# A list-scheduled attention-plus-feed-forward kernel: later landings in the planner, one more weight pair prepared during attention

## The chip, the cores and the metric

The kernel runs on one core of a Trainium2 chip. The metric is the device time of one execution in microseconds. The kernel before takes 1083.32 us (median of three runs, 1082.94 to 1085.74).

The engines are named as the profile names them: PE is the matrix engine (PEld its weight loads), DVE the vector engine, ACT the scalar engine, POOL the GpSimd engine, SP the engine whose queue issues nearly all transfers. Each executes its own instructions strictly in the order in which they stand in the program and waits on semaphores for the others.

## The reference

```python
scores = scale * np.matmul(q, k.transpose(0, 1, 3, 2))     # 8 batches x 8 heads, 576 positions, 64 wide
mask = block_i >= block_j                                  # blocks of 64: block-causal
attn = softmax(np.where(mask, scores, -1e9))
x = np.matmul(attn, v)                                     # reshaped to 4608 tokens x 512
h = x @ w_in                                               # 512 -> 2048
g = np.maximum(h, 0.0) + alpha * np.minimum(h, 0.0)        # one alpha per column of w_in
out = g @ w_out                                            # 2048 -> 512
```

The inputs q, k and v are float32. The two weight matrices arrive as float64 bit patterns and are turned into float32 on the chip.

## The kernel before, in words

**Arithmetic.** Every float32 operand of a matrix product is split into a rounded high part and a low rest (`split`, and `QH`/`QL`, `KH`/`KL`, `gh`/`gl`, `xh`/`xl`), and a product is made of three passes on PE: high by high, high by low, low by high.

**Two stages.** The 2048 hidden columns are 16 slices of 128. In the first stage, up to about 560 us, the attention of 32 head pairs is done (`query_tile` for scores, softmax and transposes, `values` for the product with v), and beside it `chunk_a` takes the finished tokens through the first six slices (`FA = 6`; `ffn1` at L638, `activate` at L649 to L659, `ffn2` at L672) in chunks of 256 tokens. After the last attention tile some chunks of `chunk_a` remain; they fill PE until about 628 us. In the second stage the other ten slices are done as five pairs by a scheme of seven instead of eight block products (`pair1` at L736, `chunk2` at L794). It needs seven combinations ("factors") of the 256 by 256 blocks of each pair of weight slices, high and low parts of each. This is what "pair" means for weights below: (1, g) are the W2 factors of pair g, from w_out, and (0, g) the W1 factors, from w_in.

**Weights.** `to_f32` loads 512 KB of float64 bits into a buffer `raw` (two exist) and makes float32 of them in a buffer `m` (two exist beside the attention) with one operation on ACT (L495) and five on DVE (L492, L497, L501, L504, L507). For the first six slices the result is split into `wa` and stays on chip. For the five pairs, `weights_ahead(p)` does it beside the attention after head pair p: two conversions, four block sums on DVE (L530), four splits on ACT (L557) and POOL (L558), and eight transfers (L562) that write the factors to DRAM (`wd` for W2, `wd1` for W1). The buffers `m` and `raw` are free again only when these transfers have landed. The table `AHEAD` says at which head pair which factors are made; its priority is `5*p + WOFF`. Pair (0, 0) is not in the table: its W1 factors are made at the change of stages, on ACT and POOL, from buffers on chip (`later_weights`); for the other four a load of 896 KB per part (L594) brings them back from DRAM.

**Order.** No order is written by hand. `Plan.op` records each operation with an engine, a cost, its buffers and a priority (lower is sooner). `Plan.schedule` is a list scheduler: it plays the program through with these costs, gives each free engine the ready operation with the lowest priority, and the order in which it does so is the order of the instructions on each engine. For a transfer it assumes that issuing takes `ISSUE`, that data begin to move `BEGINS` later, one transfer after the other at `PER_KB`, and that it has landed `LANDS` after that. What is planned too early then waits in order at run time, and all that stands behind it on that engine waits too. `slack` adds time to one operation before the next may use its result, but for transfers it is overwritten. The planned times decide order alone; the chip does not see them.

**The start.** For the first four head pairs q and k of the first 256 positions are loaded into regions of `xT` (L931, L932), k is scaled on DVE (L917) or POOL (L919), and the scores come directly from them (L1002). Values `vraw` come by L938.

Of the kernel before, what the change touches and what calls it, by code (L numbers as in the profile page):

```python
# [9 lines left out]
F32 = mybir.dt.float32  # L10
# [18 lines left out]
NG = (NF - FA) // 2  # L29
# [8 lines left out]
HALVES = (((4, 3, 2), (2 * P, S, 1)), ((1, 0), (0, 2 * P, 0)))  # L38
BANKS, HB, AB, HT, AM, AT, WB = 7, 2, 2, 5, 2, 3, 4
SLACK = 0  # L40
# [3 lines left out]
STARTS1, STARTS2 = (5, 22, 34, 46, 58), (0, 12, 17, 29, 41, 53, 65)  # L44
C0, C1 = 3.0, 4.0
WARM, WARM_END = 10, 3400
TICK, FULL_COLUMNS = 3413.33, 3060
LAG = 7.25
NORM, GL, XLA, KON = ("POOL",) * 5, ("POOL",) * 4, ("POOL",) * 2, "POOL"
W1A, W1L, WAA, WAL = ("POOL",) * 4, ("POOL",) * 4, "DVE", "POOL"  # L50
Q2B = 1
VP, VL, VE = 2.0, 2.0, 0.0
E0, E1 = -4.0, 2.0
RAW0, FIXED = -9.4, 3
NEAR, LP = 4.0, 1.0
FP = -1
# [3 lines left out]
ON_DVE, D0 = (3,), 12  # L60
WOFF, COFF = 100, 60
AHEAD = {**{8 + 4 * k: (1, k) for k in range(NG)}, **{6 + 4 * k: (0, k) for k in range(1, NG)}}
CONV = {}
SHIFTS = {}
SOON, XB = 150, 1006.7
FEW = 12
# [9 lines left out]
       ("POOL", "SP"): 120}  # L76
HELD, PACE = {"DVE": 40, "POOL": 80}, 1.012
QUEUES = ("SP", "ACTQ", "POOLQ")
ISSUE, BEGINS, LANDS, PER_KB, LANES = 430, 1300, 1000, 4.1, 8

# [19 lines left out]
class Plan:  # L100
# [45 lines left out]
    def schedule(self):  # L146
# [44 lines left out]
        while events:  # L191
# [13 lines left out]
            for engine in sorted(ready, key=lambda e: (e in ("DVE", "POOL"), since.get(e, t), ready[e][0] if ready[e] else (0, 0))):  # L205
# [54 lines left out]
                if engine in QUEUES:  # L260
                    begin = max([t, *lands[-LANES:][:len(lands) >= LANES]])
                    end = begin + ISSUE
                    pipe = max(begin + BEGINS, pipe) + cost * PER_KB
                    lands.append(pipe + LANDS)
                    lat = lands[-1] - end
                busy[engine] = end
# [90 lines left out]
def attn_ffn(ctx, tc, qT, kT, vT, w_in, w_out, alpha, out):  # L357
# [120 lines left out]
    def to_f32(src, prio, after=(), use="att", early=None):  # L478
# [9 lines left out]
        def e():  # L488
            return eb().bitcast(I32)
        op("SP", 512, lambda: nc.sync.dma_start(out=raw(), in_=src), r=after, w=[raw], prio=prio if early is None else early)  # L490

# [43 lines left out]
    def weights_ahead(p):  # L535
# [18 lines left out]
        def parts(src, n, keys, at):  # L554

            n2 = 256 * n
            op("ACT", c_act(n2, True), lambda: nc.scalar.copy(out=word(2, n).bitcast(F32R), in_=src()), r=keys, w=[hk], prio=pr)  # L557
            op(WAL, c_pool(n2) if WAL == "POOL" else c_ss(n2), lambda: (nc.gpsimd if WAL == "POOL" else nc.vector).tensor_tensor(  # L558
                out=src().bitcast(F32R), in0=src(), in1=word(2, n), op=ALU.subtract), r=[hk], w=keys, prio=pr)
            for x, v, r in ((0, lambda: word(2, n), [hk]), (1, src, keys)):  # L560
                to = wd[at:at + n, :, g, x].rearrange("m p n -> p m n") if side else wd1[g, :, x, at:at + n]
                op("SP", 128 * n, lambda to=to, v=v: nc.sync.dma_start(out=to, in_=v().rearrange("p (m n) -> p m n", n=256)),  # L562
                   r=r, w=[("wd", side, at + i, g, x) for i in range(n)], prio=pr)
        if side:
# [308 lines left out]
    def store(acc, to, t, key):  # L873
        o = Buf("o")
        op("ACT", c_act(512), lambda: nc.scalar.copy(out=o(), in_=acc()), r=[acc], w=[o], prio=FP)
        op("SP", 256, lambda: nc.sync.dma_start(out=to[t:t + P, :], in_=o()), r=[o], w=[(key, t)], prio=FP)

# [5 lines left out]
    def prep(p, pr):  # L883
# [3 lines left out]
        QH, QL, KH, KL, Q, K = (Buf(k) for k in ("QH", "QL", "KH", "KL", "Q", "K"))  # L887
        op("SP", 320, lambda: nc.sync.dma_start(out=raw(), in_=qT[p]), w=[raw], prio=pr)
        op("SP", 288, lambda: nc.sync.dma_start(out=kraw(), in_=kT[p]), w=[kraw], prio=pr)
        op("SP", 320, lambda: nc.sync.dma_start(out=vraw(), in_=vT[p]), w=[(vraw, 0), (vraw, 1)], prio=pr + VL)  # L890
        v_parts = vraw, [(vraw, 0), (vraw, 1)]
# [10 lines left out]
        def move(to, of, key, src, kb=128):  # L902
            op("SP", kb, lambda: nc.sync.dma_start(out=to().bitcast(F32), in_=of().bitcast(F32)), r=[src], w=[key], prio=pr)
        for h in range(2):
# [239 lines left out]
    def spill(b, pr):  # L1144
        r0 = (b * S) % RING
        n = S
        op("SP", 2 * n, lambda: nc.sync.dma_start(out=xd[:, :, b * S:b * S + n], in_=xT[:, :, r0:r0 + n]),
           r=xs(b), w=[("xd", b)], prio=pr)

# [14 lines left out]
    for p in range(NPAIR):  # L1164
        pr = p * 5
        qk_parts, v_parts = prep(p, pr - 4.5) if p >= NP else rest(p, pr - 4.5)
        halves = HALVES[:1] if p < NP else HALVES
        js = [j for js, _ in halves for j in js]
        for k, j in enumerate(js):
            query_tile(p, qk_parts, j, pr + k)  # L1170
        values(p, v_parts, [span for _, span in halves], pr + len(js) + VAL)
        weights_ahead(p)
        if p % NP == NP - 1:
            b = p // NP
            spill(b, p * 5 + 20)
# [114 lines left out]
```

## Time and profile before

| | |
|---|---|
| median of three runs | 1083.32 us |
| profiled execution: own time / span in the trace | 1084.71 us / 1082.9 us |
| PE idle over the span | 18.9 us (1082.9 less 1064.0 busy) |
| first matmul of the scores | 5.93 us |
| last attention product, first matmul of the second stage | 563 us, 628.65 us |
| transfers | 248 MB, 229 GB/s on average |

A row of the view of windows gives, for a stretch, its length and then for each engine the busy time and the number of instructions, then the granted clock of PE, the busy share of the sixteen DMA engines and their rate. A row of the timeline gives start, duration, engine, line, operation, output and inputs, count, and in brackets how long the engine had been idle and what released it. A row of waits gives who waited for whom, microseconds in total, how often, and the longest.

### The profile page before, as it was taken

The numbers are of one execution on the slowest core, as the hardware profiler recorded it, in microseconds if no ns is written. First come the engines' busy times: TensorE is split into PE (matmuls) and PEld (weight loads), VectorE is DVE, ScalarE is ACT, GpSimd is POOL, SyncE is SP. The second block draws the span as 40 slices with busy tenths as digits, with TensorE's granted clock in tenths as the row PEclk, the third lists the DMA queues.
The fourth block names the chain that finished last, engine by engine and source line by source line (L and its number), as shares of the span: only waits on it lengthen the run. The fifth ranks groups of instructions, "written<-read, shape, count | busy, mean of one in ns | idle before, by whom it ended". The sixth has DMA issues, their size and how long they took to land.

```text
span 1082.9 us, 24707 instructions
## 1 busy us (share of the span) xinstructions
PE 1064.0 (98%) x8158; PEld 964.8 (89%) x8158; DVE 769.5 (71%) x1731; ACT 704.1 (65%) x1977; POOL 686.9 (63%) x877
## 2 busy tenths in 40 slices
PE   7999999999999999999999999999999999999998
PEld 4678887888888887888888999999999999999998
DVE  7887775857675757686767259687777869686865
ACT  6889987676767666676754446556565656565553
POOL 4767857566767556667556616675767666675741
PEclk9999999999999999999999999999999999999999
DMA  6598988768877769668547367787877879686974
GB/s 193 185 248 240 260 253 226 244 176 235 241 214 236 198 211 272 207 191 267 161 159 288 107 253 224 224 275 230 265 249 238 268 218 285 214 286 211 296 259 156
DMA packets 150224, 248.07 MB, mean 229 GB/s; under 512 B 15952, under 2 KB 62800, under 8 KB 150096
## 3 DMA queue, kind: packets, MB, share of 16 engines
q1 hardware_dynamic: 149520, 245.96, 73.9%
q8 instruction: 65, 1.06, 0.4%
q14 instruction: 63, 0.52, 0.2%
q10 hardware_dynamic: 576, 0.52, 0.1%
HBM read 157.56 MB, written 44.83 MB: 187 GB/s over the span
## 4 chain that ended last, share of the span: by engine, by line
PE 85%; DVE 6%; ACT 4%; DMA 3%; issue 1%; POOL 1%; SPq 0%; DVEq 0%; ACTq 0%; POOLq 0%
PE bank L794 20%; PE bank L736 20%; PE bank L638 12%; PE bank L672 12%; PE bank L1134 7%; PE bank L1035 5%; PE bank L997 5%; DMA raw<-in_w_in 2%; PE bank L1065 2%; PE bank L1090 1%; ACT p L1021 1%; DVE nm L1018 1%; DVE bank L497 1%; ACT PTF L1110 1%; DMA wd<-m 0%
## 5 line engine op out<-in xcount | busy, mean ns | idle before, releaser
L736 PE MATMUL bank<-X,w 128*128 128x256 f32 x1890 | 245.6, 282 | 0.7 <-ACT g L745 0.7
L736 PEld LDWEIGHTS bank<-X,w 128*128 128x128 f32 x1890 | 233.6, 189 | 1.3 <-ACT g L745 1.1
L794 PE MATMUL bank<-w,gh 128*128 128x256 f32 x1260 | 229.2, 280 | 0.8 <-ACT gh L513 0.8
L514 POOL TENSOR_TENSOR gl<-c,gh 128x256 fp32r<-128x256 f32 x175 | 150.6, 873 | 82.6 <-ACT gh L513 64.1
L968 POOL TENSOR_SCALAR p<-p,ri 128x256 f32<-128x256 f32 (+3 forms) x256 | 142.8, 571 | 94.7 <-DVE ri L1027 51.2
L794 PEld LDWEIGHTS bank<-w,gh 128*128 128x128 f32 x1260 | 193.9, 189 | 1.0 <-ACT gh L513 1.0
L794 PE MATMUL bank<-w,gl 128*128 128x256 f32 x630 | 177.2, 281 | 0.0
L1021 ACT ACTIVATE p<-bank,nm 128x256 f32<-128x256 f32 (+3 forms) x256 | 134.6, 535 | 47.5 <-DVE nm L1018 30.2
L672 PE MATMUL bank<-wa,gh 128*128 128x512 f32 x432 | 140.5, 406 | 0.5 <-POOL wa L514 0.5
L638 PE MATMUL bank<-xh,wa 128*128 128x256 f32 x864 | 129.1, 288 | 0.3 <-ACT PTF L1110 0.3
L794 PEld LDWEIGHTS bank<-w,gl 128*128 128x128 f32 x630 | 118.9, 189 | 0.0
L659 POOL TENSOR_TENSOR gl<-g,gh 128x256 fp32r<-128x256 f32 x108 | 83.0, 770 | 55.5 <-ACT gh L655 47.2
L638 PEld LDWEIGHTS bank<-xh,wa 128*128 128x128 f32 x864 | 113.5, 190 | 3.5 <-ACT PTF L1110 0.9
L1035 PE MATMUL bank<-ident,p 128*128 128x128 f32 x640 | 100.7, 278 | 7.5 <-POOL p L968 3.2
L753 ACT ACTIVATE g<-bank 128x256 f32<-128x256 f32 x135 | 51.6, 384 | 82.7 <-DVE bank L749 67.7
L513 ACT CAST gh<-c 128x256 fp32r<-128x256 f32 x192 | 76.4, 406 | 35.4 <-PE bank L794 31.5
L1134 PE MATMUL bank<-PTF,vraw 128*64 128x320 f32 (+3 forms) x768 | 94.8, 386 | 0.0
L1035 PEld LDWEIGHTS bank<-ident,p 128*128 128x128 f32 x640 | 74.6, 142 | 21.0 <-POOL p L968 9.4
L997 PE MATMUL bank<-K,Q 128*128 128x512 f32 (+1 forms) x448 | 92.4, 327 | 0.1
L1018 DVE TENSOR_REDUCE nm<-bank 128x1 f32<-128x384 f32 (+3 forms) x144 | 81.0, 587 | 15.2 <-PE bank L997 7.8
L672 PEld LDWEIGHTS bank<-wa,gh 128*128 128x128 f32 x432 | 75.0, 189 | 12.6 <-POOL wa L514 0.8
L672 PE MATMUL bank<-wa,gl 128*128 128x512 f32 x216 | 85.2, 394 | 0.0
(180 smaller groups left out, 2135.6 us busy)
## 6 DMA issues: line engine op xcount, KB each, us to landing
w<-wd SPq DMA_DIRECT2D x315, 256.0 KB, 4.0
Q<-QH SPq DMA_DIRECT2D x56, 256.0 KB, 3.8
K<-KH SPq DMA_DIRECT2D x112, 128.0 KB, 3.5
vraw<-in_v SPq DMA_DIRECT2D x32, 320.0 KB, 4.2
qraw<-in_q SPq DMA_DIRECT2D x30, 320.0 KB, 4.0
xd<-xT SPq DMA_DIRECT2D x8, 1152.0 KB, 6.8
part<-o SPq DMA_DIRECT2D x36, 256.0 KB, 3.6
wd<-raw SPq DMA_DIRECT2D x36, 256.0 KB, 3.5
```

The source lines that it names most:

```text
L514: op(on, c_pool(n) if on == "POOL" else c_ss(n), lambda: (nc.gpsimd if on == "POOL" else nc.vector).tensor_tensor(out=lo(), in0=src(), in1 ...
L638: nc.tensor.matmul(hp()[:, :n], ww()[:, 0, cc * P:(cc + 1) * P], x()[:, cc, :n], start=(i == 0 and cc == 0), stop=(i == 2 and cc == NCC - 1))
L659: op(on, c_pool(CHA) if on == "POOL" else c_ss(CHA), lambda: (nc.gpsimd if on == "POOL" else nc.vector).tensor_tensor(out=gl(), in0=g(), i ...
L672: nc.tensor.matmul(acc(), a()[:, ts], ww(), start=(first and i == 0), stop=(last and i == 2))
L736: nc.tensor.matmul(bank()[:, :CHA], W()[:, i, 256 * at + P * c:256 * at + P * c + P], B()[:, j, CHA * c:CHA * c + CHA], start=(first and n ...
L794: nc.tensor.matmul(bank()[:, CHA * i:CHA * i + CHA], a()[:, P * i:P * i + P], W()[:, x], start=(first and g + i + n == 0), stop=(g == NG - ...
L968: op(on, 244 + n / 1.2 if on == "POOL" else c_dve2(n), lambda: e.tensor_scalar(out=t()[:, cols], in0=t()[:, cols], scalar1=by(), scalar2=1 ...
L997: nc.tensor.matmul(o, Q()[:, i, qs], K()[:, 2 * h + i, :w], start=(i == 0), stop=(i == 1))
L1018: op("DVE", c_dve(w), lambda h=h: nc.vector.tensor_reduce(out=nm()[:, h:h + 1], in_=sb[h]()[:, off[h]:off[h] + w], axis=AX.X, op=ALU.max, ...
L1021: op("ACT", 238 + w / 1.2, lambda h=h, t=t: nc.scalar.activation(out=t()[:, :w], in_=sb[h]()[:, off[h]:off[h] + w], func=AF.Exp, bias=nm() ...
L1035: nc.tensor.transpose(out=tp()[:, base + c * P:base + (c + 1) * P], in_=pts[h]()[:, c * P:(c + 1) * P], identity=ident)
L1134: nc.tensor.matmul(ob()[rows[h], a - q0:q1 - q0], V()[:, c, h, :], moving, start=(c == 0), stop=(c == cs[-1][0]))
```

## The change

Constants of the planner and of the placement, and one term in the planner's treatment of transfers:

- A transfer now lands `LANDS = 2000` after its data instead of 1000, and a transfer's `slack` is added. `LATE[1] = 2000` is the slack of the factors that go out (L562), `LATE[4] = 3000` that of the stored partial sums (L876) and of the attention's spilled result (L1147); the other three entries are zero. For a factor block of 256 KB the planner thus counts 1300 + 256 x 4.1 + 1000 = 3350 ns from the start of the issue before, and 1300 + 1050 + 2000 + 2000 = 6350 ns now.
- `AHEAD` holds all ten factor sets. The first is made after head pair 6 instead of 8. `WOFF` goes from 100 to 0, so that a conversion has the priority of the attention tiles of its time instead of one that comes behind all of them.
- The fourth entry of `GL` is DVE: for slice 3 of the first six, the low part `gl` is made on DVE instead of POOL (18 of 108 such operations).
- Loads of a head pair have priority `5*p - 5.5` instead of `- 4.5`, values no longer two later. `E0`, `E1`, `C0`, `C1`, `XB`, `SOON` move the first tiles, the first six slices' weights and the first loads of the second stage. `HT` lets four instead of five hidden banks be in use once the attention ends.

```diff
-BANKS, HB, AB, HT, AM, AT, WB = 7, 2, 2, 5, 2, 3, 4
+BANKS, HB, AB, HT, AM, AT, WB = 7, 2, 2, 4, 2, 3, 4
-C0, C1 = 3.0, 4.0
+C0, C1 = 6.0, 3.0
-NORM, GL, XLA, KON = ("POOL",) * 5, ("POOL",) * 4, ("POOL",) * 2, "POOL"
+NORM, GL, XLA, KON = ("POOL", "POOL", "POOL", "POOL", "POOL"), ("POOL", "POOL", "POOL", "DVE"), ("POOL", "POOL"), "POOL"
-VP, VL, VE = 2.0, 2.0, 0.0
-E0, E1 = -4.0, 2.0
+VP, VL, VE, PP = 3.0, 0.0, 0.0, 5.5
+E0, E1 = -3.0, 0.6
-WOFF, COFF = 100, 60
-AHEAD = {**{8 + 4 * k: (1, k) for k in range(NG)}, **{6 + 4 * k: (0, k) for k in range(1, NG)}}
+WOFF, COFF = 0, 60
+AHEAD = {6: (1, 0), 8: (0, 0), 10: (1, 1), 12: (0, 1), 15: (1, 2), 17: (0, 2), 19: (1, 3), 22: (0, 3), 24: (1, 4), 26: (0, 4)}
-SOON, XB = 150, 1006.7
+SOON, XB = 140, 1004.7
+LATE = (0, 2000, 0, 0, 3000)
-ISSUE, BEGINS, LANDS, PER_KB, LANES = 430, 1300, 1000, 4.1, 8
+ISSUE, BEGINS, LANDS, PER_KB, LANES = 430, 1300, 2000, 4.1, 8
@@ schedule @@
-                    lat = lands[-1] - end
+                    lat = lands[-1] - end + lat
@@ weights_ahead, parts @@
-                   r=r, w=[("wd", side, at + i, g, x) for i in range(n)], prio=pr)
+                   r=r, w=[("wd", side, at + i, g, x) for i in range(n)], prio=pr, slack=LATE[1])
@@ store; spill likewise @@
-        op("SP", 256, lambda: nc.sync.dma_start(out=to[t:t + P, :], in_=o()), r=[o], w=[(key, t)], prio=FP)
+        op("SP", 256, lambda: nc.sync.dma_start(out=to[t:t + P, :], in_=o()), r=[o], w=[(key, t)], prio=FP, slack=LATE[4])
@@ attn_ffn @@
-        qk_parts, v_parts = prep(p, pr - 4.5) if p >= NP else rest(p, pr - 4.5)
+        qk_parts, v_parts = prep(p, pr - PP) if p >= NP else rest(p, pr - PP)
```

One line is added near the top, so that line numbers of the changed kernel are one higher below it. On PE the last 3541 matmuls, from about 658 us on, stand in the same order in both kernels.

**First place: the first transfers on SP.** Before:

```order
L938 DMA vraw_156<-in_v 128x256
L938 DMA vraw_159<-in_v 128x256
L932 DMA xT<-in_q 128x256 x3
L931 DMA xT<-in_k 128x256
L932 DMA xT<-in_q 128x256
L490 DMA raw_169<-in_w_in 128x1024
```

Now:

```order
L933 DMA xT<-in_q 128x256 x3
L932 DMA xT<-in_k 128x256
L933 DMA xT<-in_q 128x256
L491 DMA raw_164<-in_w_in 128x1024
L939 DMA vraw_166<-in_v 128x256
L939 DMA vraw_169<-in_v 128x256
```

The two loads of values have moved from the head of the queue to behind the first load of weights; the first q is now the first transfer.

**Second place: ACT around the second use of `m` by the first factor set (1, 0).** `m_242` is the first of the two buffers in both; `CAST raw<-m` splits a factor out of it, and the next `ACTIVATE bank<-m` works on the following conversion in the same buffer. Before:

```order
L898 CAST KH_716<-kraw_171 128x576
L1021 ACTIVATE p_201,s_133<-bank_194,nm_204 128x512
L1021 ACTIVATE p_207,s_133<-bank_176,nm_204 128x512
L557 CAST raw_169<-m_293 128x512
L495 ACTIVATE bank_231<-m_242,ebias 128x512
L1138 COPY xT<-bank_145 128x320
L1110 COPY PT_109<-bank_194 64x128
```

Now:

```order
L876 COPY o_1307<-bank_231 128x512
L558 CAST raw_164<-m_344 128x512
L1111 COPY PTF_108<-bank_190 128x4x128
L1111 COPY PTF_108<-bank_180 128x4x128
L1111 COPY PTF_108<-bank_173 128x3x128
L1111 COPY PTF_108<-bank_192 128x3x128
L1022 ACTIVATE p_197,s_139<-bank_145,nm_200 128x128
L1022 ACTIVATE p_204,s_139<-bank_145,nm_200 128x128
L496 ACTIVATE bank_180<-m_242,ebias 128x512
```

The step on the reused buffer stood directly behind the cast of the other buffer, and six rows of attention now stand between. Counted from the cast of `m_242` itself it is 13 rows before and 19 now.

**Third place: SP where the two loads for the first factor set stand.** Before:

```order
L888 DMA qraw_174<-in_q 128x640
L890 DMA vraw_156<-in_v 128x640
L889 DMA kraw_171<-in_k 128x576
L490 DMA raw_169<-in_w_out 128x1024
L490 DMA raw_192<-in_w_out 128x1024
L876 DMA part<-o_1199 128x512
```

Now:

```order
L904 DMA Q_129<-QH_687 64x2x512
L891 DMA vraw_166<-in_v 128x640
L491 DMA raw_164<-in_w_out 128x1024
L491 DMA raw_215<-in_w_out 128x1024
L904 DMA Q_129<-QL_731 64x512
L904 DMA K_131<-KH_719 64x512 x2
```

Eight loads of `qraw` by L888 stood before these two loads, and five stand before them now: they come three head pairs earlier, among the moves of Q and K.

More of the change, by code (lines that the diff above doesn't have):

```diff
@@ L48 @@
 LAG = 7.25
-NORM, GL, XLA, KON = ("POOL",) * 5, ("POOL",) * 4, ("POOL",) * 2, "POOL"
-W1A, W1L, WAA, WAL = ("POOL",) * 4, ("POOL",) * 4, "DVE", "POOL"
+NORM, GL, XLA, KON = ("POOL", "POOL", "POOL", "POOL", "POOL"), ("POOL", "POOL", "POOL", "DVE"), ("POOL", "POOL"), "POOL"
+W1A, W1L, WAA, WAL = ("POOL", "POOL", "POOL", "POOL"), ("POOL", "POOL", "POOL", "POOL"), "DVE", "POOL"
 Q2B = 1
-VP, VL, VE = 2.0, 2.0, 0.0
-E0, E1 = -4.0, 2.0
+VP, VL, VE, PP = 3.0, 0.0, 0.0, 5.5
+E0, E1 = -3.0, 0.6
 RAW0, FIXED = -9.4, 3
@@ L489, in e @@
             return eb().bitcast(I32)
-        op("SP", 512, lambda: nc.sync.dma_start(out=raw(), in_=src), r=after, w=[raw], prio=prio if early is None else early)
+        op("SP", 512, lambda: nc.sync.dma_start(out=raw(), in_=src), r=after, w=[raw], prio=prio if early is None else early, slack=LATE[0] if after else 0)
         op("DVE", c_dve2(512), lambda: nc.vector.tensor_scalar(
@@ L887, in prep @@
         QH, QL, KH, KL, Q, K = (Buf(k) for k in ("QH", "QL", "KH", "KL", "Q", "K"))
-        op("SP", 320, lambda: nc.sync.dma_start(out=raw(), in_=qT[p]), w=[raw], prio=pr)
-        op("SP", 288, lambda: nc.sync.dma_start(out=kraw(), in_=kT[p]), w=[kraw], prio=pr)
-        op("SP", 320, lambda: nc.sync.dma_start(out=vraw(), in_=vT[p]), w=[(vraw, 0), (vraw, 1)], prio=pr + VL)
+        op("SP", 320, lambda: nc.sync.dma_start(out=raw(), in_=qT[p]), w=[raw], prio=pr, slack=LATE[3])
+        op("SP", 288, lambda: nc.sync.dma_start(out=kraw(), in_=kT[p]), w=[kraw], prio=pr, slack=LATE[3])
+        op("SP", 320, lambda: nc.sync.dma_start(out=vraw(), in_=vT[p]), w=[(vraw, 0), (vraw, 1)], prio=pr + VL, slack=LATE[3])
         v_parts = vraw, [(vraw, 0), (vraw, 1)]
@@ L902, in move @@
         def move(to, of, key, src, kb=128):
-            op("SP", kb, lambda: nc.sync.dma_start(out=to().bitcast(F32), in_=of().bitcast(F32)), r=[src], w=[key], prio=pr)
+            op("SP", kb, lambda: nc.sync.dma_start(out=to().bitcast(F32), in_=of().bitcast(F32)), r=[src], w=[key], prio=pr, slack=LATE[2])
         for h in range(2):
@@ L1147, in spill @@
         op("SP", 2 * n, lambda: nc.sync.dma_start(out=xd[:, :, b * S:b * S + n], in_=xT[:, :, r0:r0 + n]),
-           r=xs(b), w=[("xd", b)], prio=pr)
+           r=xs(b), w=[("xd", b)], prio=pr, slack=LATE[4])
     early_loads()
```

## The prediction

> **What bounds the kernel now.** I read the busy times first, then the windows, then the waits of PE, then the timeline at the two largest of these waits.
>
> ```profile
> PE 1064.0 (98%) x8158; PEld 964.8 (89%) x8158; DVE 769.5 (71%) x1731; ACT 704.1 (65%) x1977; POOL 686.9 (63%) x877
> ...
> 0.00:20.00 20.00, 14.15 (x80) 8.56 (x82) 12.27 (x51) 12.15 (x34) 8.16 (x25) 1.00 0.63 206
> 20.00:40.00 20.00, 18.16 (x124) 11.11 (x122) 18.62 (x57) 16.77 (x55) 14.03 (x20) 1.00 0.60 191
> 40.00:60.00 20.00, 19.45 (x147) 13.48 (x143) 17.79 (x44) 18.27 (x50) 14.99 (x20) 1.00 0.61 180
> 60.00:100.00 40.00, 37.45 (x259) 30.89 (x258) 32.15 (x81) 32.27 (x90) 28.42 (x37) 1.00 0.93 254
> 100.00:200.00 100.00, 97.69 (x746) 82.98 (x744) 67.13 (x183) 81.18 (x249) 63.98 (x89) 1.00 0.88 252
> 550.00:600.00 50.00, 49.98 (x333) 44.09 (x332) 34.80 (x61) 26.40 (x66) 27.40 (x33) 1.00 0.64 234
> 700.00:800.00 100.00, 100.00 (x847) 100.00 (x846) 75.41 (x138) 59.62 (x155) 68.31 (x81) 1.00 0.79 250
> ```
>
> PE is busy 1064.0 of 1082.9 us; no other engine comes near. In the second stage (700 to 800 us) it is never idle. The change neither adds nor removes a matmul, so time can come only out of PE's 18.9 idle microseconds, or out of slow matmuls, or be lost by new idle time. 5.85 us of the idle lie in the first 20 us, 2.55 in 60 to 100, 2.31 in 100 to 200. At the change of stages, 550 to 600 us, there is nothing to win: 49.98 of 50. What ended PE's waits:
>
> ```profile
> PE bank L1035 <- POOL p L968: 3.2, 5, 2.0
> PE bank L1002 <- DMA xT<-in_q: 2.5, 1, 2.5
> PE bank L1035 <- ACT PT L1110: 2.3, 1, 2.3
> PE bank L1035 <- DVE g L651: 1.1, 1, 1.1
> PE bank L736 <- ACT g L745: 0.7, 2, 0.5
> ```
>
> Two single waits stand out: 2.5 us for the first q and 2.3 us for a PT. Both are of a kind that the change touches.
>
> **Term 1, the start.** Here are the first transfers, what they release, and two equal groups of matmuls either side of 17 us.
>
> ```profile
> 0.74 0.88 SPq L938 DMA_DIRECT2D vraw<-in_v  x2
> 1.66 1.37 SPq L932 DMA_DIRECT2D xT<-in_q  x3
> 3.38 0.29 DVE L917 TENSOR_SCALAR xT<-xT 128x256 f32<-128x256 f32 x1 [1.64 <-DMA xT<-in_k]
> 5.81 0.33 SPq L490 DMA_DIRECT2D raw<-in_w_in  x1
> 5.93 1.23 PE L1002 MATMUL bank<-xT 64*128 64x256 f32 x4 [2.52 <-DMA xT<-in_q]
> 6.91 0.78 POOL L919 TENSOR_SCALAR xT<-xT 128x256 f32<-128x256 f32 x2 [4.46 <-DMA xT<-in_k]
> 10.93 0.69 PE L1035 MATMUL bank<-ident,p 128*128 128x128 f32 x2 [2.01 <-POOL p L968]
> 16.11 1.55 PE L1134 MATMUL bank<-PTF,vraw 128*64 128x256 f32 x8
> 19.71 0.87 PE L1134 MATMUL bank<-PTF,vraw 128*64 128x256 f32 x8
> ```
>
> The first scores wait for q alone: its k is there at 3.38 and scaled at 3.67, while q, issued behind two loads of values, comes at 5.9. Now q is first in the queue. The transfers that have that place before take 2.6 us to land, the slowest of the first 12 us takes 5.7:
>
> ```profile
> vraw<-in_v SPq DMA_DIRECT2D x2, 128.0 KB, 2.6
> xT<-in_q SPq DMA_DIRECT2D x1, 256.0 KB, 5.7
> ```
>
> So q lands at about 0.74 + 2.6 = 3.3, k is scaled at 3.7, and with some 0.2 us from k to PE the first scores start at 3.9 instead of 5.93: 2.0 us sooner. The values, moved behind the first load of weights, are used only at 16.11 (then 14.1); the weight load ahead of them went out at 5.81 in the old order, so that even with 5.7 us to land they are there by about 12.5. POOL scales k of the third and fourth pair (end 7.7) ahead of its first softmax scaling, which it did before 10.93 and would now do 2 us sooner, so it just fits.
>
> Not all of the 2.0 us reach the end. The same eight matmuls of L1134 take 1.55 us at 16.11 and 0.87 at 19.71, a factor of 0.56; around 17 us PE changes its pace. If that moment stays where it is, the 2.0 us won before it are filled with slow work, worth 2.0 x 0.56 = 1.1 us; if it moves along with the work, all 2.0 are kept. I take 1.6, the middle, and keep 1.1 and 2.0 as ends.
>
> [...]
>
> **Term 2, the outgoing factor at 182 us.**
>
> ```profile
> 178.56 0.62 ACT L557 CAST raw<-m 128x512 fp32r<-128x512 f32 x1 [1.78 <-DMA wd<-raw]
> 181.64 0.55 SPq L562 DMA_DIRECT2D wd<-m  x1
> 186.82 1.60 DVE L492 TENSOR_SCALAR m<-raw 128x512 int32<-128x512 int32 x1 [1.67 <-DMA wd<-m]
> 188.51 0.69 ACT L495 ACTIVATE bank<-m,ebias 128x512 int32<-128x512 int32 x1 [3.31 <-DVE m L492]
> 189.45 0.25 ACT L1110 COPY PT<-bank 64x128 f32<-64x128 f32 x1
> 189.70 0.63 PE L1035 MATMUL bank<-ident,p 128*128 128x128 f32 x4 [2.31 <-ACT PT L1110]
> ...
> 181.64 5.09 DMA wd<-m
> ...
> wd<-m SPq DMA_DIRECT2D x18, 256.0 KB, 4.3
> ```
>
> The chain is read from below. PE waits for the PT that ACT copies at 189.45; ACT stood 3.31 us before L495; that waited for DVE, which may not write `m` before its old content has landed in DRAM, 5.09 us after the issue. The planner believed 3.35 us from issue to landing; the median measured is 4.3. Now it counts 6.35, above both. In the new order 19 rows of ACT instead of 13 stand between the cast of this buffer and its next use. Before, those 13 rows ran from 178.56 to 185.2 without a pause (188.51 less the wait of 3.31), 0.51 us each; six more put L495 3.1 us later among its neighbours, which nearly covers the 3.31. So the 2.31 us of PE go, and at most a few tenths stay. The other end is 0: the same wait comes back somewhere among the ten conversions, of which the tightest beside the attention has 16 rows. I take 2.3, since a plan with 6.35 us leaves ACT its slack in time even where rows are few.
>
> **Edits that I cost at nothing.** The fifth W1 pair leaves the change of stages. There ACT has 26.40 busy of 50, POOL 27.40, and PE is full of `chunk_a`; had the cover gone, the longest of these steps would count:
>
> ```profile
> L514 POOL TENSOR_TENSOR w<-m,w 128x512 fp32r<-128x512 f32 x2 | 3.0, 1524 | 0.0
> L659 POOL TENSOR_TENSOR gl<-g,gh 128x256 fp32r<-128x256 f32 x108 | 83.0, 770 | 55.5 <-ACT gh L655 47.2 <-PE bank L638 7.5 <-POOL gl L659 0.5
> L514 DVE TENSOR_TENSOR gl<-c,gh 128x256 fp32r<-128x256 f32 x17 | 7.3, 432 | 4.2 <-ACT gh L513 4.1
> ```
>
> Two more loads of factors are added there, issued 60 us ahead of their use. The 18 `gl` on DVE take 18 x 0.770 = 13.9 us from POOL and give 18 x 0.432 = 7.8 us to DVE, both spread over 600 us and under 72% busy; if each were on the path it would be 0.34 us shorter, 6 us at most. `HT`, `SOON` and `XB` act where PE has no idle time; the 0.7 us at L736 I leave in place. The new order of the small attention tiles between 20 and 100 us changes waits of about 5 us in sum (2.4 us in 20 to 60 and 2.55 above), all of half a microsecond to one; each may vanish or have a new twin. I take 0 and keep 3 either way.
>
> **Sum.** The profiled execution took 1084.71 us around its span of 1082.9. Less 1.6 and 2.3 that is 1080.8. It lay 1.39 above the median of the runs, so against the median: 1083.32 - 3.9 = 1079.4 us.
>
> **Rivals.** The first factor set is now made three head pairs earlier, from about 105 us on instead of here:
>
> ```profile
> 141.89 0.90 SPq L490 DMA_DIRECT2D raw<-in_w_out  x2
> ...
> 100.00:120.00 20.00, 20.00 (x173) 17.17 (x172) 13.01 (x39) 19.31 (x64) 13.46 (x20) 1.00 0.90 233
> 120.00:140.00 20.00, 20.00 (x147) 16.22 (x147) 14.36 (x47) 17.80 (x58) 17.47 (x25) 1.00 0.97 268
> ...
> L495 ACT ACTIVATE bank<-m,ebias 128x512 int32<-128x512 int32 x32 | 22.4, 705 | 7.5 <-DVE m L492 5.5 <-DVE sp L1025 1.6 <-DVE ri L1027 0.4
> L557 ACT CAST raw<-m 128x512 fp32r<-128x512 f32 x18 | 11.3, 631 | 3.1 <-DMA wd<-raw 2.0 <-POOL m L558 1.2
> ```
>
> (a) *ACT becomes the bound there.* One conversion of a pair costs ACT 2 x 0.705 + 3 x 0.631 + 0.4 = 3.7 us, and in 100 to 140 us it has 0.69 + 2.20 = 2.9 free. Between 0.8 and 3.7 us would fall on PE. For it: 19.31 of 20. Against it: the scheduler can give PE more of the feed-forward there, which asks less of ACT. With 2.3 us lost: 1081.7, no change that could be told.
>
> (b) *Slower: the transfers clog.* The pair brings 2 x 512 KB in and 14 blocks of 128 KB out, 2.8 MB, at 250 GB/s 11 us of all DMA engines. At the share of 0.88 of this hundred microseconds, some 50 us have 6 us free. The other 5 us push back the moves of Q and K, which stand in the same queue and without which there are no scores; and with all transfers late the wait of term 2 stays. Then 1083.32 - 1.6 + 5 = 1086.7 us. It decides once a move lands more than some 5 us later than now; below that the feed-forward products that PE has at hand cover it. Against it: no PE wait before 560 us names a DMA but the very first, though the share was 0.97 in one window.
>
> (c) *The change does only one of its two things*: the stall at 182 us reappears (1081.7), or the start is held by another load (1081.0). No difference that could be told.
>
> (d) *More*: half of the small waits of 20 to 100 us go as well, 1079.4 - 2.5 = 1076.9.
>
> **Chances.** The forecast 0.43, (a) and (c) together 0.29, (b) 0.12, (d) 0.16. About 0.3%, 3.25 us, is what a measurement of this kernel can tell from none; faster by that means below 1080.07. Of the forecast, whose own range is 1077 to 1082, some two thirds lie there (0.29), of (d) all (0.16), of (a) and (c) a quarter (0.07): faster 0.52. Slower is (b), 0.12, and 0.36 is left for no change. The range goes from 1074.5 (both terms at their upper ends, 4.3 us, and the 5 us of small waits gone) to 1085.5 (into rival b).
>
> **What would show it.** Term 1: the first L1003 matmul at 3.9 us and the first L1036 at 8.9; wrong if PE still waits for q or k past 5 us. Term 2: no wait of PE over 1 us between 100 and 560 us, and DVE before L493 never over a microsecond on a landing. Rival (a): ACT at 95% or more and PE idle between 100 and 140 us. Rival (b): PE waiting for scores whose K or Q landed late, the DMA share at 1.0 from 100 to 150 us. The prediction is wrong as a whole if PE's idle time in the trace is not between 11 and 20 us, or if its busy time moves by more than 2 us.

## The result and the profile after

The changed kernel takes 1080.80 us (median of 7 runs, 1079.34 to 1081.21); the kernel before, run beside it, 1085.74 us (7 runs, 1082.94 to 1092.27). The ratio is 0.9946, with a 95% interval of 0.9922 to 0.9971: faster by 0.54%. The prediction was 1079.4 us in a range of 1074.5 to 1085.5, "faster" the likeliest. Over all comparisons reported here the kernel before ran 84 times, with medians of 1084.9 to 1085.8 us, so the 1083.32 of the first three runs, from which the prediction started, was some 1.6 to 2.4 us low.

The profiled execution of the changed kernel took 1081.21 us around a span of 1079.2, against 1084.71 and 1082.9. Its busy times, from the page:

```profile
PE 1065.4 (99%) x8158; PEld 967.4 (90%) x8158; DVE 768.4 (71%) x1753; ACT 704.9 (65%) x1977; POOL 669.6 (62%) x855
```

Its windows:

```profile
0.00:20.00 20.00, 14.19 (x74) 8.59 (x75) 11.48 (x48) 12.06 (x35) 7.76 (x25) 1.00 0.65 209
20.00:100.00 80.00, 77.22 (x553) 57.75 (x553) 71.66 (x185) 67.59 (x194) 58.14 (x74) 1.00 0.72 213
100.00:560.00 460.00, 459.88 (x3359) 395.06 (x3356) 320.36 (x836) 336.92 (x1000) 297.72 (x395) 1.00 0.78 227
560.00:700.00 140.00, 139.52 (x1025) 131.99 (x1024) 82.63 (x165) 70.43 (x184) 66.04 (x79) 1.00 0.67 235
```

The same stretches of the kernel before:

```profile
20.00:100.00 80.00, 75.07 (x524) 55.48 (x521) 68.56 (x180) 67.31 (x193) 57.44 (x75) 1.00 0.77 220
100.00:560.00 460.00, 456.98 (x3341) 391.67 (x3340) 314.49 (x814) 331.68 (x994) 301.76 (x403) 1.00 0.75 220
560.00:700.00 140.00, 139.48 (x1035) 131.37 (x1034) 88.94 (x164) 73.05 (x186) 76.40 (x90) 1.00 0.64 219
```

PE's idle time is the length of a stretch less its busy time. It fell from 18.9 to 13.8 us. In the first 20 us nothing changed (5.81 against 5.85), from 20 to 100 us 2.78 are left of 4.93, from 100 to 560 us 0.12 of 3.02, and the change of stages is as before (0.48 against 0.52). Against the 5.1 us stand 1.4 us of more busy time, which leaves the 3.7 of the span.

What PE still waits for:

```profile
PE bank L1036 <- POOL p L969: 4.7, 2, 4.4
PE bank L473 <- DVE warm L369: 1.1, 1, 1.1
PE bank L795 <- ACT gh L514: 0.8, 1, 0.8
PE bank L639 <- POOL xl L627: 0.7, 1, 0.7
```

The 2.5 us for q and the 2.3 us for a `PT` are gone. The first row is new in its size: one wait of 4.4 us, at the start. The timeline there:

```profile
3.08 0.43 SPq L491 DMA_DIRECT2D raw<-in_w_in  x1
3.08 0.36 ACTq L932 DMA_DIRECT2D xT<-in_k  x1
3.78 1.23 PE L1003 MATMUL bank<-xT 64*128 64x256 f32 x4 [0.38 <-DVE xT L918]
9.66 0.94 POOL L920 TENSOR_SCALAR xT<-xT 128x256 f32<-128x256 f32 x2 [7.20 <-DVE ri L1028]
10.59 2.54 POOL L969 TENSOR_SCALAR p<-p,ri 128x256 f32<-128x256 f32 x6
11.12 1.15 PE L1036 MATMUL bank<-ident,p 128*128 128x128 f32 x4 [4.35 <-POOL p L969]
15.85 1.55 PE L1135 MATMUL bank<-PTF,vraw 128*64 128x256 f32 x8
20.37 0.87 PE L1135 MATMUL bank<-PTF,vraw 128*64 128x256 f32 x8
```

And from the view of the tile `xT` over the first 12 us, how long its loads took:

```profile
DMA to landing us min/median/max: 2.3/3.7/6.5
```

The first scores start at 3.78 us as forecast, but the first transposes at 11.12, later than the 10.93 of before. POOL stood until 9.66 before its scaling of k (L920), and the softmax scalings (L969) stand behind that in order. The bracket names a reciprocal of DVE (`ri`), but L920 reads nothing of it: it needs the third load of k, issued at 3.08 and landed at 9.57, the 6.5 us of this row. Before, that load was issued at 3.10 and landed at 6.83. What is new beside it is a load of 512 KB of weights, issued in the same microsecond; before, that went out at 5.81.

### The profile page after: what moved, and what is told of

Same layout as the page of the kernel before. It is cut to its first block, busy times and chain, and to the rows that moved or that the text cites. A ratio compares the mean times of both kernels' runs of the same rounds, so it can differ in the third digit from the quotient of the medians.

```text
span 1079.2 us, 24731 instructions
## 1 busy us (share of the span) xinstructions
PE 1065.4 (99%) x8158; PEld 967.4 (90%) x8158; DVE 768.4 (71%) x1753; ACT 704.9 (65%) x1977; POOL 669.6 (62%) x855
## 4 chain that ended last, share of the span: by engine, by line
PE 92%; DVE 2%; ACT 2%; issue 1%; POOL 1%; DMA 0%; DVEq 0%; POOLq 0%; ACTq 0%
PE bank L795 19%; PE bank L737 19%; PE bank L673 14%; PE bank L639 14%; PE bank L1135 8%; PE bank L998 6%; PE bank L1036 6%; PE bank L1066 2%; PE bank L1091 1%; PE bank L1003 1%; ACT p L1022 0%; ACT PTF L1111 0%; PE bank L1100 0%; DVE xb L692 0%; POOL gl L515 0%
## 5 line engine op out<-in xcount | busy, mean ns | idle before, releaser
L969 POOL TENSOR_SCALAR p<-p,ri 128x256 f32<-128x256 f32 (+3 forms) x256 | 140.4, 563 | 80.0 <-DVE ri L1028 54.4
L639 PE MATMUL bank<-xh,wa 128*128 128x256 f32 x864 | 128.7, 287 | 0.0
L639 PEld LDWEIGHTS bank<-xh,wa 128*128 128x128 f32 x864 | 114.1, 190 | 2.7 <-issue 0.7
L660 POOL TENSOR_TENSOR gl<-g,gh 128x256 fp32r<-128x256 f32 x90 | 69.7, 777 | 69.0 <-ACT gh L656 48.3
L514 ACT CAST gh<-c 128x256 fp32r<-128x256 f32 x193 | 76.7, 407 | 34.7 <-PE bank L795 30.6
L1135 PE MATMUL bank<-PTF,vraw 128*64 128x320 f32 (+3 forms) x768 | 94.9, 386 | 0.1
L1019 DVE TENSOR_REDUCE nm<-bank 128x1 f32<-128x384 f32 (+3 forms) x144 | 81.0, 587 | 19.7 <-PE bank L998 14.9
L652 DVE SCALAR_TENSOR_TENSOR g<-g,oal,bank 128x256 f32<-128x256 f32 x108 | 51.5, 477 | 53.3 <-ACT g L650 52.5
L1111 ACT COPY PTF<-bank 128x384 f32<-128x384 f32 (+2 forms) x152 | 72.2, 504 | 23.0 <-PE bank L1036 22.2
```

The lines of the kernel that those rows point to most:

```text
L514: op("ACT", c_act(n, True), lambda: nc.scalar.copy(out=hi(), in_=src()), r=r, w=[hk], claim=claim, prio=prio)
L639: nc.tensor.matmul(hp()[:, :n], ww()[:, 0, cc * P:(cc + 1) * P], x()[:, cc, :n], start=(i == 0 and cc == 0), stop=(i == 2 and cc == NCC - 1))
L969: op(on, 244 + n / 1.2 if on == "POOL" else c_dve2(n), lambda: e.tensor_scalar(out=t()[:, cols], in0=t()[:, cols], scalar1=by(), scalar2=1 ...
L1019: op("DVE", c_dve(w), lambda h=h: nc.vector.tensor_reduce(out=nm()[:, h:h + 1], in_=sb[h]()[:, off[h]:off[h] + w], axis=AX.X, op=ALU.max, ...
L1135: nc.tensor.matmul(ob()[rows[h], a - q0:q1 - q0], V()[:, c, h, :], moving, start=(c == 0), stop=(c == cs[-1][0]))
```

## The experiments

### The start

Theory: the weight load held the third k, that held POOL, and POOL the transposes. The kernel `s_start` is the changed kernel with that load moved behind the two first loads of values; each engine but SP keeps its order.

```diff
-        for _, i in self.schedule():
+        order = [i for _, i in self.schedule()]
+        loads = [i for i in order if self.ops[i][0] == "SP"]
+        weight, value = loads[5], loads[7]
+        order.remove(weight)
+        order.insert(order.index(value) + 1, weight)
+        for i in order:
             self.ops[i][2]()
```

> The changed kernel with one load moved: the first 512 KB of weights is issued on SP behind the two first loads of values instead of ahead of them; every engine's own order stays. Theory: in the changed kernel the third load of k landed 6.5 us after its issue because that weight load, issued in the same microsecond, shared the DMA engines with it, and POOL's scaling of that k (in order ahead of the softmax scalings) then held the first transposes to 11.1 us. So here the third k lands by about 7 us, POOL begins its second k scaling by 7.7 us, the first transposes begin near 8.9 us, and the kernel is 1.1 to 2.3 us faster than the changed one. Rival: the first transposes wait for the DVE's reciprocals, as the view of waits names them; then they stay near 11.1 us and the time stays within 0.5 us of the changed kernel's. Second rival: the transposes move up, but the pace of TensorE, which rose only near 19.6 us, eats the gain, or the later weight load is now waited for near 12 to 20 us; then first transposes near 8.9 us and a gain under 0.5 us.

Measured: 1079.19 us (6 runs, 1078.26 to 1080.31), ratio to the kernel before 0.9933 (0.9906 to 0.9959). Its start (line numbers are five higher):

```profile
2.97 0.37 ACTq L937 DMA_DIRECT2D xT<-in_k  x1
6.77 0.78 POOL L925 TENSOR_SCALAR xT<-xT 128x256 f32<-128x256 f32 x2 [4.33 <-DMA xT<-in_k]
8.67 0.69 PE L1041 MATMUL bank<-ident,p 128*128 128x128 f32 x2 [2.04 <-POOL p L974]
13.86 0.87 PE L1140 MATMUL bank<-PTF,vraw 128*64 128x256 f32 x8
```

The third k landed at 6.69, the transposes start 2.45 us sooner, and the median is 1.6 us lower. The profiled span is 3.0 us shorter, which overstates it: that execution is the fastest of its kernel, the changed kernel's the slowest of its own. So the theory of the wait holds and the first rival falls. The medians speak against the second, a gain under 0.5 us. But the intervals of the two kernels overlap, so the size of the gain is less sure than its cause.

`s_q_first` asks the same of the kernel before: q first, but no weights ahead of the values.

```diff
-        for _, i in self.schedule():
+        order = [i for _, i in self.schedule()]
+        loads = [i for i in order if self.ops[i][0] == "SP"]
+        values, to = loads[:2], loads[7]
+        order = [i for i in order if i not in values]
+        at = order.index(to)
+        order[at:at] = values
+        for i in order:
             self.ops[i][2]()
```

> The kernel before with the two first loads of values moved on SP behind the four first loads of q, ahead of the first load of weights; every other engine's order stays. This is the prediction's first term alone, without the weight load that the changed kernel put ahead of the values. Theory: first scores near 3.8 us instead of 5.9, first transposes near 8.8 instead of 10.9, and 1.1 to 2.0 us of it kept: the profiled execution's excess of PE at 40 us falls by 1 to 3 us against the kernel before; the medians, which spread over 10 us here, can show it only roughly (1082.5 to 1085). Rival: PE gains nothing because the slow pace of its first matmuls lasts as long after the first transposes as before; then the excess at 40 us stays within 0.7 us.

Measured: 1083.72 us (12 runs), ratio 0.9982 (0.9966 to 0.9998). The first scores start at 3.70 us and the first transposes at 8.73, as the theory has it. The same scores further on, in the kernel before and, six lines lower, in this one:

```profile
32.59 1.13 PE L1002 MATMUL bank<-xT 64*128 64x512 f32 x4
```

```profile
30.40 1.13 PE L1008 MATMUL bank<-xT 64*128 64x512 f32 x4
```

2.2 us sooner, just above the 1.1 to 2.0 of the theory. The medians give 1.2 us, with an interval from 0.2 to 3.7. So the first term was sound as a mechanism, and nothing here speaks against its size; the changed kernel's order withheld it.

### The stall at 190 us

`s_reuse` is the kernel before with one conversion step moved, the one that waited for `wd<-m`. The fifteenth L492 and its two dependents (L495, L497) go behind the three copies of `PTF` that stood behind it on DVE.

```diff
...
+        late = [steps[14]]
+        at = order.index(late[0])
...
+        to = order.index(copies[2])
+        for i in order[at + 1:to]:
+            if self.ops[i][3] & set(late):
+                late.append(i)
+        order[at:to + 1] = [i for i in order[at:to + 1] if i not in late] + late
```

> The kernel before with one step moved: the conversion step whose result goes into the tile that a late transfer still reads (the fifteenth of its kind) stands on DVE behind the three copies of transposed probabilities, with its two dependents; all other order is the kernel before's. Theory: this one wait cost the PE's 2.31 us at 189.7 us; it goes, and the kernel is about 2.3 us (0.2%) faster than the kernel before in its profiled execution's PE idle, with no PE wait over 0.5 us between 180 and 200 us. Rival: the step's own consumer, ScalarE's exponential and the matmuls of the next pair's map, is late next, so a wait of 1 us or more comes back within 50 us and the time moves under 0.8 us.

Measured: 1084.78 us (12 runs), ratio 0.9996 (0.9978 to 1.0014): nothing that can be told. In its timeline (lines ten higher) the step no longer waits:

```profile
191.04 0.42 DVE L502 TENSOR_SCALAR m<-raw 128x512 int32<-128x512 int32 x1
```

PE's waits between 180 and 200 us are now one, for something else:

```profile
PE bank L1045 <- POOL p L978: 1.3, 1, 1.3
```

1.3 us of the 2.3 come back at 196.5 us, where softmax tiles are now late: the rival, in part. And `s_q_first`, whose orders of DVE, ACT, POOL and PE are those of the kernel before, shows what that wait is worth in another execution. Its row for the same stretch:

```profile
PE bank L1041 <- ACT PT L1116: 0.3, 1, 0.3
```

The same place of the program costs 2.31 us in one execution and 0.3 in another. Everything there lies some 2 us earlier, the factor block lands after 4.57 instead of 5.09 us, and the step behind it takes 0.87 instead of 1.60 us. A second place shows the same. In the kernel before and in `s_reuse`, whose orders are equal up to the moved step, DVE waits for the same weight load:

```profile
61.93 0.69 DVE L501 TENSOR_SCALAR bank<-raw 128x512 int32<-128x512 int32 x1 [1.49 <-DMA raw<-in_w_in]
```

```profile
64.14 0.69 DVE L511 TENSOR_SCALAR bank<-raw 128x512 int32<-128x512 int32 x1 [3.50 <-DMA raw<-in_w_in]
```

Issued at 55.25 and 55.46, it landed after 6.7 and 8.7 us, and PE's wait behind it was 1.1 and 3.1 us. A plan that counts 4.4 us for it (1.3 + 512 x 0.0041 + 1.0) is at the mercy of such differences.

### The landing edit and the fifth pair

Four kernels part these two edits from the rest: the landing edit alone, the table of pairs alone (`WOFF` and `AHEAD`), both, and the changed kernel without the pairs. A fifth is the changed kernel without the landing edit.

The landing edit is the lines `LATE` and `LANDS` of the change, with the three `slack=` and the `+ lat`; the table of pairs is its lines `WOFF` and `AHEAD`. `s_land_undone` is the changed kernel with `LANDS` 1000 and `LATE` all zero, `s_ahead` the changed kernel with the old `WOFF` and `AHEAD`.

> The kernel before with the planner's landing edit alone (2000 instead of 1000 ns for every transfer, 2000 more for the outgoing W1 factors, 3000 more for the outgoing intermediate rows), all placements, loads and pairs as before. Theory: the landing edit is what removes the 2.31 us stall at 190 us and the small ones between 313 and 484 us (1.3 us), so PE idle between 100 and 560 us is under 0.5 us, and the kernel is 2.5 to 4 us faster than before, at 1079.5 to 1081.5 us, with a spread of runs as narrow as the changed kernel's (under 3 us) where the kernel before spread over 9 us. Rival: the fifth pair, the moved loads and the placements did it; then a stall of over 1 us stands in 100 to 560 us and the gain is under 1.5 us.

> The changed kernel with the planner's landing edit alone undone (1000 ns for every transfer, nothing more for outgoing ones). Theory: waits for landings come back in 100 to 560 us, PE idle there is 2 us or more with at least one DVE wait for a transfer of over 3 us, and the kernel is 2 to 4 us slower than the changed one, near the kernel before, with runs spread over more than 4 us. Rival: other edits carry the gain; then PE idle in 100 to 560 us stays under 0.7 us and the time within 1 us of the changed kernel's.

> The changed kernel with the table of W1 pairs alone set back: the two factor sets start at different times and the pair (0,0) is made at the change of stages again; landing figures, start, placements as changed. Theory: the landing edit and the move of the fifth pair need each other. With the landing edit alone the kernel before lost 40 us, 31 of them in two PE waits (16.1 us at 574 us and 14.9 us at 644 us) where conversions of a pair stood in order ahead of the work of the change of stages and waited for outgoing factors to land; so here PE waits of over 5 us come back between 560 and 670 us, and the time is 1095 us or more. Rival: the 40 us came from other numbers left at their old values (how many tiles the conversions share, the loads' order at the change of stages), and the move of the pair is worth nothing, as predicted; then the time is within 3 us of the changed kernel's 1080.8 us.

> The kernel before with the table of W1 pairs alone changed (both factor sets side by side from the start, all five pairs beside the attention), landing figures and all else as before. Theory: the pairs need the longer landing figures; without them conversions beside the attention wait for transfers, as in the changed kernel with its landing edit undone (1091.0 us, 5 us of PE idle between 100 and 560 us), so 1086 to 1093 us and PE idle of 3 us or more in 100 to 560 us. Rival: the pairs alone bring the gain; then under 1083 us.

> The kernel before with the landing edit and the table of W1 pairs together, and nothing else of the change (start order, tile counts, placements and loads at the change of stages as before). Theory: these two carry the gain behind 20 us; PE idle in 100 to 560 us under 0.7 us, no PE wait over 2 us between 560 and 670 us, 1080 to 1084 us. Rival: the placements and tile counts are needed too; then PE waits of over 3 us stand between 560 and 670 us, or the time is above 1087 us.

Measured, with PE's idle time in three stretches (us) of each profiled execution:

| kernel | landing | pairs | rest | median us | runs us | 20–100 | 100–560 | 560–700 |
|---|---|---|---|---|---|---|---|---|
| before | old | old | old | 1084.9–1085.8 | 1082.1–1093.0 | 4.93 | 3.02 | 0.52 |
| `s_land_only` | new | old | old | 1125.25 | 1124.5–1126.8 | 4.39 | 0.35 | 37.01 |
| `s_pairs_only` | old | new | old | 1088.67 | 1084.2–1092.9 | 5.32 | 1.34 | 0.52 |
| `s_land_pairs` | new | new | old | 1084.54 | 1084.0–1085.7 | 4.38 | 0.83 | 2.18 |
| `s_ahead` | new | old | new | 1121.81 | 1119.9–1122.8 | 2.64 | 2.26 | 34.40 |
| `s_land_undone` | old | new | new | 1090.99 | 1088.1–1092.9 | 6.38 | 5.01 | 0.00 |
| after | new | new | new | 1080.80 | 1079.3–1081.2 | 2.78 | 0.12 | 0.48 |

The profiled execution of `s_pairs_only` is the fastest of its runs, 4.5 us under their median, so its idle times are at the low end.

The theory for `s_land_only` was wrong by some 45 us, in its total. Its guess for 100 to 560 us holds (0.35 us), but at the change of stages 37 us are lost. DVE's timeline of `s_land_only` there, with the row of PE that it holds up:

```profile
574.81 0.42 DVE L531 TENSOR_TENSOR raw<-m,raw 128x256 f32<-128x256 f32 x1 [0.36 <-DMA wd<-raw]
582.26 0.87 DVE L493 TENSOR_SCALAR m<-raw 128x512 int32<-128x512 int32 x1 [7.03 <-DMA wd<-m]
588.98 0.43 DVE L493 TENSOR_SCALAR m<-raw 128x512 int32<-128x512 int32 x1 [3.08 <-DMA raw<-in_w_in]
589.91 0.35 DVE L624 CAST xh<-xT 128x128 fp32r<-128x128 f32 x2
590.19 2.07 PE L639 MATMUL bank<-xh,wa 128*128 128x256 f32 x8 [16.13 <-DVE xh L624]
```

A pair's conversions stand on DVE ahead of a cast that takes 0.35 us, and their two landings, 10.1 us of waiting, keep `xh` and with it PE for 16.1 us. A second wait, 14.9 us for `w`, follows when the pair (0, 0) is made. `s_ahead` loses the same way (16.1 and 12.2 us), so the tile counts and loads of the change of stages do not cure it, and the move of the pairs does: 1125.25 to 1084.54 without the rest, 1121.81 to 1080.80 with it, 41 us both times. Where the landing figures are old, the same move costs 2.9 us by the medians: 1088.67 against 1085.75, ratio 1.0027 (1.0008 to 1.0046). Its time is as the theory had it; the 3 us of idle expected from 100 to 560 us are not in this execution (1.34). What makes the planner leave the conversions in that place when landings are longer is open.

`s_land_undone` is 10.2 us slower than the changed kernel, where the theory said 2 to 4. The idle time from 100 to 560 us came back as expected (5.01), but so did as much as 6.38 us from 20 to 100, which it had not counted.

`s_land_pairs` meets neither the theory's 0.7 us in 100 to 560 us (0.83) and 1080 to 1084 us in all, nor the rival's 3 us waits; it takes 1084.54 us, ratio 0.9981 (0.9967 to 0.9995). So these two edits together bring 1.2 us by the medians, and the remaining 3.7 come from the other constants or from the order in which all of them happen to result.

### How much is the order's luck

Three kernels change one figure of the planner a little, with everything else as changed: `LANDS` is 2100 in `s_nudge`, 1900 in `s_1900`, and 1100 in `s_1100`, there with `LATE` all zero.

```diff
-ISSUE, BEGINS, LANDS, PER_KB, LANES = 430, 1300, 2000, 4.1, 8
+ISSUE, BEGINS, LANDS, PER_KB, LANES = 430, 1300, 2100, 4.1, 8
```

> The changed kernel with the landing figure at 2100 instead of 2000 ns, everything else as changed. It measures what any new roll of the order costs. Theory: the gain comes from the margin that the figure gives, so 5% more of it changes the order but keeps the time within 2 us of 1080.8. Rival: each new order by itself moves the time by 3 us or more, up or down, and the changed kernel's gain is a lucky order as much as a margin; then outside 1078.5 to 1083.5 us.

> The changed kernel with the landing figure at 1900 instead of 2000 ns. At 2100 it took 1086.2 us, 5.4 more than at 2000, from single waits of 1 to 3 us at 88 to 130 us. Theory after that: each order is a draw, with the longer figure the draws lie between 1079 and 1087 us and their runs spread under 4 us; so here 1079 to 1087, spread under 4 us, and not below 1079. Rival: 2000 sits on a slope (a smaller figure is better, a larger worse); then below 1080.

> The changed kernel with the landing figure at 1100 and nothing more for outgoing transfers: a second draw of the kernel without the landing edit, which at 1000 took 1091.0 us with runs over 4.7 us. Theory: short figures cost time and spread whatever the draw; so 1085 to 1092 us, runs spread over 4 us or more, PE idle of 2 us or more in 100 to 560 us. Rival: 1091.0 was an unlucky draw and the landing edit is worth nothing in the mean; then 1079 to 1084.5 us.

Measured: 2100 gives 1086.16 us (10 runs, 1084.21 to 1087.78), 1900 gives 1094.90 (5 runs, 1092.57 to 1095.92), 1100 gives 1092.87 (10 runs, 1088.70 to 1094.80). Five per cent of the figure, up or down, costs 5.4 and 14.1 us. Both theories fell: the time does not stay within 2 us, and the draws reach beyond 1087. `s_1100` is near what was expected of it: 0.9 us above its range of 1085 to 1092, its runs 6.1 us apart, PE idle 3.99 us from 100 to 560 us. Most of the loss at 2100 and 1900 arises between 20 and 100 us, where PE is idle 6.54 us at 2100 and 11.66 at 1900, against 2.78. The largest wait there at 2100, from PE's timeline:

```profile
84.78 1.17 PE L998 MATMUL bank<-K,Q 128*128 128x384 f32 x7
89.04 0.66 PE L1036 MATMUL bank<-ident,p 128*128 128x128 f32 x4 [3.09 <-POOL p L969]
91.09 1.75 PE L1036 MATMUL bank<-ident,p 128*128 128x128 f32 x7 [1.22 <-POOL p L969]
```

The windows behind it:

```profile
88.00:92.00 4.00, 1.74 (x11) 1.55 (x12) 3.28 (x11) 3.42 (x9) 3.65 (x5) 0.76 1.07 236
92.00:96.00 4.00, 4.00 (x20) 3.98 (x19) 3.49 (x10) 3.32 (x10) 3.30 (x5) 0.50 0.81 200
```

No landing ends this wait. In the chain of work ahead of it two conversion steps of the first weights stand on DVE between softmax steps (L493 and L502, from 86.43 to 87.36 us). They are worth at most 0.9 of the 3.09 us; what made the softmax steps late besides is open. At 1900 a conversion is named directly: PE's longest wait there, 2.6 us, ends with `wa` from ACT (L514). After the wait at 2100 the row reads a granted clock of 0.50, and single matmuls of L1066 (128x288) take 0.44 us from 93.31 on, where the changed kernel's take 0.29 to 0.32 on average: some slow work came with the wait besides.

What does follow the landing figures is the spread of the runs. With 1900 or more, whatever else differs (eight kernels), the runs of a kernel have a standard deviation of 0.5 to 1.3 us; with 1000 or 1100 (six kernels) 1.6 to 3.1 us. Between 100 and 560 us those with the longer figures idle 0.1 to 2.3 us, the others 1.3 to 5.0. So a longer figure goes with a steadier kernel and mostly with less waiting beside the attention, but whether the whole is faster hangs on the order between 20 and 100 us.

### HT, SOON and XB

`s_late_stage` is the changed kernel with these three set back; all order ahead of the change of stages stays.

```diff
-BANKS, HB, AB, HT, AM, AT, WB = 7, 2, 2, 4, 2, 3, 4
+BANKS, HB, AB, HT, AM, AT, WB = 7, 2, 2, 5, 2, 3, 4
-SOON, XB = 140, 1004.7
+SOON, XB = 150, 1006.7
```

> The changed kernel with HT, SOON and XB set back together; all order ahead of the change of stages stays, and some 15 to 36 rows per engine move behind it. Theory, the prediction's own: these numbers act where PE has no idle time, so the time stays within 0.5 us of the changed kernel's 1080.8. Rival: with all five pairs beside the attention they are what keeps PE fed behind the change of stages; the kernel before with the landing figures and pairs alone lost 2.2 us between 600 and 700 us where the changed kernel lost 0.5; then 1.2 to 2 us slower, 1082 to 1083.

Measured: 1081.07 us (10 runs, 1080.13 to 1082.40), 0.3 above the changed kernel: the prediction's own zero. Its ratio to the kernel before, 0.9958 (0.9941 to 0.9974), lies within the changed kernel's interval. Yet PE is idle 1.71 us between 560 and 700 us instead of 0.48, through

```profile
PE bank L737 <- ACT g L746: 1.3, 2, 0.8
```

a wait that the changed kernel does not have in this stretch. So they save 1.2 us of idle time in one trace and 0.3 in the medians, less than the 2 us by which the runs of either kernel spread: neither the zero nor the rival is settled.

## Why the prediction was right in its number and not in all its steps

**Term 1, the start, gave nothing in the trace.** The first scores came as worked out (3.78 for 3.9). The 0.2 us counted from k to PE was an estimate that no run shows; in the changed kernel they began 0.06 us after the end of k's scaling, at 3.72. The step that failed is "POOL scales k of the third and fourth pair (end 7.7) [...] so it just fits": it took the landing of the third k, 6.83, from the old order, though the same paragraph had the first weights go out ahead of the values. That load was asked only whether the values would suffer. Of the seven profiled executions that begin with the weights so early, none had the third k before 7.75 us (7.75 to 9.91); in the seven others it was there at 6.59 to 6.98. With the load out of the way the 1.6 us forecast are about what the medians give (1.2 and 1.6).

**Term 2 went as forecast, on weaker ground than it seemed.** No wait of PE over 1 us is left between 100 and 560 us, and DVE never stands 0.3 us before L493. The landing edit alone clears this stretch too (`s_land_only`, 0.35 us idle); that the plan's 6.35 us for a factor block is what does it, and not the order as a whole, is argued, since a plan with 0.1 us more has a wait of 1.1 us there (at 129.8, for a `PT`). And 2.31 us was one execution's value of a wait that another execution of the same order on the engines had at 0.3. Here a single profile priced the stall only to within its own size.

**An edit at nothing made up for term 1.** The small waits of 20 to 100 us, "I take 0 and keep 3 either way", gave 2.15 us here. That is more than one execution's chance: the four kernels that share PE's order up to 100 us (after, `s_start`, `s_late_stage`, `s_ahead`) idle 2.3 to 2.8 us in this stretch, the three with the order of before (before, `s_q_first`, `s_reuse`) 4.9 to 6.6. In neighbouring orders the same waits were 1.6 (at 2100) and 6.7 us (at 1900) above those of before, so a bound of 3 does not hold for such edits in general. The fifth pair was put at zero because the change of stages was covered in the profile of before; by itself it costs 2.9 us, but the landing edit without it loses 41. The prediction never asked what each edit does without the others.

**The sum** came out by luck. Forecast were 1.6 + 2.3 = 3.9 us. The spans of the two traces differ by 3.7: nothing from the start, 2.15 from 20 to 100 us and 2.90 from 100 to 560 us, less the 1.4 us of more busy time, which the prediction did not count. And the forecast was taken from 1083.32: the medians of the runs moved by 4.9, not 3.9, and the start of the count lay 2.4 too low, so that the two errors cancelled in part. Rival (c), the start held by another load, and rival (d), about half of the small waits gone, both happened. Rivals (a) and (b) did not: ACT is busy 17.5 and 15.0 of 20 us in 100 to 140 us, and no wait of PE names a move of K or Q. The tests for the whole held (PE idle 13.8 us, busy time up by 1.4).

**Open:** whether the landing edit makes the mean kernel faster, or only steadier, since the orders that it gives differ by 14 us; which of the start's and the placement's constants made the stretch of 20 to 100 us a good one, and where the 1.4 us of busy time come from. A later change of PE's pace at the start would give some: `s_start`, where it came sooner, is busy 1.2 us less.

## What to carry to other kernels

When a load moves up in a queue, look at what else lands in the same microseconds, on other queues too, and who stands in order behind that: the third k took 6.5 us to landing here instead of 3.7. With a list scheduler the gain of a change of figures need not be the stall it was made for: run neighbours of the figure before believing the sign, and read the spread of the runs as well as their median. A move that brings nothing by itself can be what another edit needs, so test edits apart and together.

## What the runs showed of the hardware

A 128 KB load of k landed 3.7 to 3.9 us after its issue beside other small loads (seven executions) and 5.0 to 6.9 us after it with a 512 KB load issued within 0.3 us of it (seven others). In `s_start`, where that one load alone was moved away, it was 3.7 again.

PE's pace at the start differed between two executions with the same order there. `s_late_stage` has that of the changed kernel; its eight matmuls of L1135 took 0.91 us already at 14.55, where the changed kernel's took 1.55 at 15.85 and 0.87 only at 20.37. In `s_start` the like eight took 0.87 at 13.86; of its 3.0 us of shorter span, 1.8 are less idle time and 1.2 less busy time (1064.2 against 1065.4). The granted clock of the row did not always go with the pace. From 12 to 14 us, `s_late_stage` and then the changed kernel:

```profile
12.00:14.00 2.00, 2.00 (x11) 1.15 (x10) 1.32 (x7) 1.66 (x6) 0.17 (x1) 0.50 0.69 235
12.00:14.00 2.00, 2.00 (x12) 1.23 (x12) 0.86 (x3) 1.09 (x4) 1.13 (x3) 1.00 0.53 202
```

About as many matmuls in the same 2 us, at 0.50 in one row and 1.00 in the other. Four matmuls of L1003 (64x256) took 1.23 us in both executions, at 12.30 and 13.60, and 0.68 in `s_late_stage` at 16.11, where its row reads 1.00 (16 to 18 us). So the 1.00 of the changed kernel's row does not tell the pace here, and the time of one form of matmul does. What the moment of the change hangs on is open.

Behind some waits of PE the granted clock read lower. In `s_land_only`, where PE was idle for 16.1 us up to 590.19, it read 0.50 also when work came back:

```profile
575.00:580.00 5.00, 0.00 (x0) 0.00 (x0) 0.23 (x1) 1.23 (x2) 2.46 (x2) 0.79 0.51 183
590.00:595.00 5.00, 4.81 (x22) 4.82 (x23) 3.81 (x10) 1.83 (x5) 2.10 (x4) 0.50 1.06 374
595.00:600.00 5.00, 5.00 (x44) 5.00 (x43) 2.04 (x4) 2.57 (x7) 2.00 (x4) 1.00 1.01 417
```

22 matmuls in the five microseconds at 0.50, 44 in the next at 1.00; eight of L639 took 2.07 us at 590.19 and 1.12 at 595.28. Shorter waits were followed by the same reading. In the 2100 kernel 3.09 us of idle up to 89.04, then 0.8 us of work and 1.22 of idle, stood ahead of the 0.50 from 92 to 96 us, and in `s_1100` 2.19 us stood ahead of this one:

```profile
75.34 0.86 PE L1091 MATMUL bank<-ident,pl 128*128 128x128 f32 x4 [2.19 <-DVE g L652]
76.00:79.00 3.00, 2.77 (x9) 1.76 (x8) 3.00 (x6) 0.98 (x3) 0.94 (x1) 0.50 1.01 226
```

In `s_reuse` a wait of 3.12 us, ended at 65.96, left the row at 1.00 (60 to 100 us), and so did the 2.31 us of before (188 to 195 us). So in these traces the length of a wait alone does not tell what the clock reads behind it: 0.50 behind 2.19 us, 1.00 behind 3.12. Behind 20 us the changed kernel waits 0.8 us at most, and its rows from 20 to 1000 us read 1.00.
